# A gated linear recurrence and a two-layer MLP on one core: all steps issued in another order

## The chip, the core and the metric

The kernel runs on one core of a Trainium2 chip. The metric is the device time of one execution in microseconds; a version's time is the median of its executions. The core has five instruction queues that matter here: PE (TensorE, matrix products), DVE (VectorE) and ACT (ScalarE) for elementwise work, POOL (GpSimd) for small elementwise work, and SP (SyncE), which in this kernel issues every DMA transfer. Each queue runs its instructions in the order in which they were written; between queues, semaphores hold an instruction back until its inputs are there and its buffer is free.

## The reference

```python
# q, k, v, a_re, a_im: (4, 8, 768, 48), that is batch, heads, tokens, width
mag = np.sqrt(a_re * a_re + a_im * a_im)
scale = np.minimum(mag, 0.999) / (mag + 1e-06)
a_re_n, a_im_n = (a_re * scale, a_im * scale)
for t in range(S):
    new_re = ar * S_re - ai * S_im          # ar, ai: row t of a_re_n, a_im_n
    new_im = ar * S_im + ai * S_re
    S_re, S_im = (new_re + kv, new_im)      # kv: outer product of k[t] and v[t]
    y[:, :, t] = np.einsum('bhd,bhde->bhe', q[:, :, t], S_re)
# y reshaped to x: (3072 tokens, 384)
h = x @ w_in                                # w_in: (384, 2048)
g = np.maximum(h, 0.0) + alpha * np.minimum(h, 0.0)
out = g @ w_out                             # w_out: (2048, 384)
```

A recurrence with a complex gate per token and channel gives y; an MLP with a leaky rectifier is applied to every token of y.

## The kernel before, in words

**Units and stages.** The tokens are cut into 24 chunks of 128 (4 batches of 6), called units. The kernel is a set of Python generators, each a chain of steps, and each step writes one or a few instructions into one engine's queue:

- nine generators `gates` (letters A to I in the order; three for batch 0, two for each later batch). A gate generator loads the complex gates of one to three chunks (L248), computes decays and phases on ACT, DVE and POOL (L251 to L425: running products in L336 and L338, the decay tree in L316) and writes them to DRAM: the decays to `decs` (L321), the phases to `phs` (L417, L427).
- `loads` (J): for each unit the queries and keys KQ (L575, L577; three buffers), the phases PP (L586; one buffer) and the decays T (L593; two buffers).
- `half_rows` (K), which rearranges the values in DRAM into `vsc` (L556), and `loads_v` (L): the values V and VL of each unit (L602 to L628).
- `pieces` (M), `weights("in")` (N) and `weights("out")` (O): the MLP's weights are loaded as raw words (L487) and converted on ACT and DVE (L503 to L515).
- 24 generators `unit` (P to Z, then a to m). DVE turns KQ by the phases (L648). Then come six levels: PE makes the products `ps_lv` (L662) of queries with a copy W of the keys (L719 on ACT), DVE multiplies KQ by the decays T (L701), and the products are masked into A (L683 on ACT, L686 on DVE). Then KQ is transposed (L736), kv products are made (L747), y is summed from the levels (L759, L768) and from the state St (L777, L780 on DVE; L793 on PE), copied out (L807) and written to DRAM (`ysc`, L812). The first unit of a batch (P, V, b, h) loads its first state (L706) and scales it (L709).
- `loads_x` (n): reads y back as xT for a group of one or two units (L825; 14 groups). `all_mlp` (o): for each group and each of 16 feature blocks the product h (L841, three matmuls), the rectifier (L848 on ACT, L850 on DVE), and the output product (L860), two output rows of chunks; the result goes through L870 and out by L873.

A level of a unit needs DVE, PE and ACT one after another; the MLP of a group needs PE most. MLP steps of earlier groups are put between the levels of later units.

**What sets the order.** The string `ORDER` (L30 to L74) has one letter for each step, 4316 in all. `Plan.run` takes the letters from left to right and advances the generator of that letter by one step. So ORDER alone sets the order of every queue: a letter writes its instructions behind all that stand before it on the same engine. The calls `DVE(...)`, `ACT(...)`, `PE(...)`, `DMA(...)` in the yields (for instance `k_ = yield DVE(H * D, ek)` in L779, a step's size and what it waits for) were read by the planner that made the string; in the kernel they all go to a function that returns None. Semaphores are placed by the framework from the tiles that are read and written, whatever the order. The DMA issues of all generators stand in SP's one queue; the listing of the built program shows that an issue also waits for the transfer eight issues earlier, since eight semaphores are used in turn.

Of the kernel before, what the change touches and what calls it, by code (L numbers as in the profile page):

```python
# [27 lines left out]


ORDER = (  # L30
    "AAAAAAAAAAAAAAAAAAAABBJBAAMMMMKMAAAAAAANNBAAAAAAAAAAAAAAABNBMAAAJAAAAAAAAAAJJBANALBABAABANBBBOBABBAB"
    "AABAAAAKAOBNABKKMBBOBBOKBBBLLLAOABBLLLLLLABMLLBABANAAAAABOABABNAAABAKBAABNNOBBBNBBBONOMLBBBBOBOBBBBB"
    "BBNBBBBNNBOBBNBBNOOOBBBBOBCBJJPCBBBBBBOBMCCCOPBJBJCBMJNBPMBNNPPBBBJPKKKKKKKKBBBCBBCBOCKCBCBCCCCPCPCK"
    "BPCPPOPJJJLJCCPNJJPNPCDDCCCCPPCPOCONCQPCOPCQPPPQPPPQPCPPQCQOCJPJPPJPPMJJNPNNNCQCQQCCOOPPPPPCPOCPCNCP"
    "PPCPNCOPCPPCJMQQLPCCQQCDCOJPCCNNMLDCONCCCCCNCCNJKMCMnKKRCCCKORNCNCJCRLJJDCCCRCCCCQCOOOCCRRCCQCOCOOMO"
    "COOCRRooooNCNKKoCooNooOKCOCLKKMKoKKDCoooCCCCooQQQQKCooRQQCCQQNQQooQDooDDLLCNoooCDQQCQoQoooooRoooQDDQ"
    "DDRLLLLLLLLDDDoDoRQRDDDCQDQDQQQRDQRJQQQEEooooRDRoooRQNEJJJoQQNQQJJQDDLDDDDSDRDROoEoooooooESSRDSDooRo"
    "NoDERRoNRoDoSDREEooooSDLLLooEDooooRRoSLLLRDDDDRooORRDDSDDEQLLLLLLLRSRDRRNRRRRDSRDDDDODDooooDDDDEoNES"
    "oJooooOSSNJJEoJRJRRRSSTLLLLLLLLooSSoooOoJRRKDDJRoELSTnOTTToSKKoDDDoooooTLoSDDDDDDDDDoSSSSoRLToEooKoT"
    "oSoooooSSoSooooooooTETDEooSLoSSLLoETDDDEDDDooooooDSoooSSSSSSTSoSJTSoDEJJEJJEKJDoooLJLDoDLLEDEEoLoSSE"  # L40
    "SSSSSTSoooJoUoTEEEEooDDooToDooooEooooooooTnLDDooooDooooooooDEUTooooooJJLDDJooooDoooEoooooooooUTooToo"
    "oLLLLLooTDTETLooooooUTEooUoTTEoDUoooTEoEUTLooTKooEUEToJToToooUETTTTTTTETEEEETJEEEFJFETUoLoUUooooooUV"
    "TLUoFoToooTTLLUUooLoToUooVFVoUoUUUUoUUoooooFoJJUUVLLTULLLLLLoooVEEEUFUVooUUUEEEooTooEEEEEEEEEEEUUVUU"
    "UJUVUVEEFooVEooooJJJJJWVooEEEEEJUoUUUVooWUVJVoUVWKWJUoUVoEVEVWoVEEJoEEEoJWWWoJJJoVVVoWVooooVWEWVVnoL"
    "LLLLoVXLLLLooooLLLEEFLVFELEEEEFoEoVooooooVVoEoWEoVoooVoooVVVVVVVVWVEVLWWWooooooJoFFWVFWWEWXFooVVWWEV"
    "WooVLLJLJVooooooooooLLLLLVFWEWWFWWFoooooooWooooVWWoooWLLLLLWWWWWoFXXFXXWEWWoFoWFXXJFJJJJLYXFoooooooo"
    "XFXXoFFFFKJJWGoWWWXooooFooooYYWYXGWWWFoXFooYXFXoooooFoYXXXYFooYFFGFoooooooooXXooYXXooXYGooFXooFXFFXo"
    "oooXXGooXXFFFoFFLnooGoGJYoGLLLLLLLLLLLLXXXXXFFFXXFFFFXFFXJYJJJJZoGoooKooYoGooJoooooooooGGoYXZYYGYFFF"
    "FFFFFFGGJZFoZoFoooZoooGGooooXYYYYXXYZZZooYYLFLLLLLLooLLLFFoLoLLZooooXXYKKFFFFYYFFZYoooooGYYoFooFFFYF"
    "LoFGYGGGFooKoJJJKKFGGGGoYYYYYYYYYJXZooooKZoJJaKKKooLFFFooZZZLoJoZLLLooFGJLLLLXLLoLoKGFFFFoFFoooooooG"  # L50
    "GGYFYZaZaaZZooZZooooGaZZFLLFJFoooooooYYYYYYooaaFoaooooaoooJooJooZaZZZaooooZoooFZnZGGaooaoGooGGooZZZZ"
    "ZZZZaZZZGJJJHaaGJbbHooooooooooooooobGaGoZGZZaaaaaJLJJabGGHZoGZZZJJbooooooGGGooGooooaLooJboaabbHHboLL"
    "ooooaboaHbLaooaooooooHooLLLoLLooLaaLLoooGGooGGbaaGGaaGGaaooGoaJGoGGGGGGGGGGGHabbcLLHaHbGcbHHHHJJJboo"
    "ooooooooJJboooobLLGGocoobobJoooobcGGGcbbbboooHoHGbccbcKJJLLLLGoooooaocLdHaLooaobaGGbcLbLKLooGGLabbba"
    "ooooooobbGbbcHbGbbboocncoooHbGGGGGGGooocHHbodoooJJoLLoHLLoLLGGGLLLGLLHoooooLLoHooHoHoooooccKdooooooH"
    "HHHHGoooooHHooodoGLHcdoocccccobbbbbbHbdJdooGooooHoodHcHdoooooooocccddocoHHHodHHJcJJJoooJcoooccocIooo"
    "odHccccccoHccdIcoodeoHJoHoodooHHHHdodHddddHccccHJeLcLJcoooLJLLLeooooooooddooccLeLJoHHooHeHHHHHHHHedd"
    "dLIeoLooodooHHddooooLLdoLLoJJdeHHHdddddIIdddonoILJodoeoooooeLooILLfoooHHHHHHoeeooJooJIooKKoooooeHHfd"
    "dfIfodLeoeLKeKfoKKoeoodoLddIdLJJffLLLLLLeeofoeeIoofeooeooooIeooIofHHIJHHIdoIIeeooJoooHHHooeKHHoIIeoe"
    "ooeeeofHHoooeHHHHeeeeeIHLILLoooeIoeJeJJffooooooooooooKeoffgJffooooooIIoooooooooLLHHooIHHIIIfeeeeegoo"  # L60
    "ofoooeegooooooooLfffffooooooofgfggJooofLfJooLfooLLfLKHgLofLLgoofogJoffffffffIgffnooogogooJJJhIIIIooL"
    "oooIIhogoohJoooohIgLfJffLLgooooofffoIggoooooooooohLhLLLIgghgIggJLgLLgJooIooooggohgoIoIghofoooooohhgI"
    "IogoIIhgooohooooooLIIILIggggggggIJJhJooJhhgLLLhhiohoooooooIIoooohhhhhooooohohJooJgIIIIIIhhLLLIIIILhI"
    "IiooLooggooggihhhIoiooogoooooohIIIILIgJLLLLLoohoooooioIIooIIIIoIoohhohhhhhhihJoJnJiiiJJJJooooooooohI"
    "IIIIIIiooIjooIIoIIioiooIoooIIIooooojijiiooooooooLoojiooooIoojhLiILLiLLIoLoooiiiiJoLLooLooohLhooooIho"
    "ihhihjjooiooooiioiijjoooiiojiLLLioiiiioooJJJjjiiiioooLoooJjjioojjojJokooooooooojjikiiijjjJJkLoooijoo"
    "oookokkjjLkoooLookojkojkoojiijjnooookojoooooooookjLLLoLooLLLLLLjjjjjJJJkJJjJLoooooLLLLLoojjjoooooooo"
    "ooooolJJLoooollLjjjkjjojkkloooooooooooooooljjLkkkkklkLkllkJooooooooooolllkLklkJJLJLoooooolLkooookook"
    "kkooooooookkkkkkkkkJJoomooooooookkmkkkloollooooooJJokmooookknloooooooooommlmLoollmlLlloooooooloLoooo"
    "ooooooomoLllmmLLLooooooooolooooooooooollloooolloooomLoLoLLLLLllllllmlmmmoomoooooooooooooollmooooolll"  # L70
    "lllmomlmmmmmLooooooooLLoLLLoooLLLooLooooooooooooooooooooooooooooooooolnooooooomooooooooooooooooomooo"
    "ooooooooooooomoooomoomooooLooLLoomooooooooommooommmmmmmmmmmmmmmnoooooooooooooooooooooooooooooooooooo"
    "oooooooooooooooooooooooooooooooooooooooooooooooooooooooooooooooooooooooooooooooooooooooooooooooooooo"
    "oooooooooooooooo")  # L74

# [27 lines left out]
def kernel(  # L103
# [33 lines left out]
    B, HP, _, D, S = q.shape  # L137
    H = 2 * HP
# [60 lines left out]
    DVE = ACT = POOL = PE = DMA = step  # L199
# [443 lines left out]
    def unit(u):  # L643
# [59 lines left out]
        if c == 0:  # L703
            k_ = yield DMA(144, *[("state", u - 2)] * (u > 1), takes=(R["St"],))
# [3 lines left out]
            k_ = yield DVE(H * D, k_, ("start", 0))  # L708
            nc.vector.tensor_tensor(out=St, in0=St, in1=start[:, b].unsqueeze(2).to_broadcast([D2, H, D]), op=ALU.mult)  # L709
            state[b] = (St, k_)  # L710
        k_ = r
        for h in LEVELS:
# [12 lines left out]
            k_ = yield DVE(2 * H * HC, e, *[("decays", u)] * (h == 1))  # L725
# [23 lines left out]
        ek = e  # L749
# [23 lines left out]
        for s in range(1 if last else 2):  # L773
            before, known = states[s]
            k_ = yield DVE(H * D, known, takes=(R["St"],))
            St = work.tile([D2, H, D], F32, tag="St", name="St", bufs=3)
            nc.vector.tensor_tensor(out=St, in0=before, in1=T[:, :, TL - 4 + s:TL - 3 + s].to_broadcast([D2, H, D]),  # L777
                                    op=ALU.mult)
            k_ = yield DVE(H * D, ek)  # L779
            nc.vector.tensor_tensor(out=St, in0=St, in1=kv[s][0:D2], op=ALU.add)  # L780
            R["lv" if s else "misc"].put(k_)
            states.append((St, k_))
# [119 lines left out]
    with tc.manual_schedule():  # L902
        for i, g in enumerate(GATES):
            plan.add(gates(i, *g))
        plan.add(loads())
        plan.add(half_rows())
        plan.add(loads_v())
        plan.add(pieces())
        plan.add(weights("in"))
        plan.add(weights("out"))  # L910
        for u in range(NU):
            plan.add(unit(u))
        plan.add(loads_x())
        plan.add(all_mlp())
        plan.run(ORDER)
# [37 lines left out]
```

## Time and profile before

| | us |
|---|---|
| median of 3 executions | 864.73 |
| lowest and highest | 863.57, 866.52 |
| the profiled execution, its own time | 865.47 |
| its span, first to last instruction | 863.5 |
| busy: PE | 707.2 |
| busy: DVE | 649.0 |
| busy: ACT | 427.4 |
| busy: POOL | 172.2 |
| DMA: 129.20 MB on SP's queue, share of 16 engines | 65.1% |

The profile is of one execution. A busy time is the time in which at least one instruction of the engine was executing; the matmuls' ends are modelled, so a busy PE is not PE at its peak. The slices of the page cut the span in 40 equal parts of 21.6 us and give the busy share of each in tenths. A wait is named by the instruction that waited, the one that released it, the total in us, how many times, and the longest. Lines (L...) are those of the kernel file. A matmul of 32-bit floats shows as two records.

### The profile page before, as it was taken

The numbers are of one execution on the slowest core, as the hardware profiler recorded it, in microseconds if no ns is written. First come the engines' busy times: TensorE is split into PE (matmuls) and PEld (weight loads), VectorE is DVE, ScalarE is ACT, GpSimd is POOL, SyncE is SP. The second block draws the span as 40 slices with busy tenths as digits, with TensorE's granted clock in tenths as the row PEclk, the third lists the DMA queues.
The fourth block names the chain that finished last, engine by engine and source line by source line (L and its number), as shares of the span: only waits on it lengthen the run. The fifth ranks groups of instructions, "written<-read, shape, count | busy, mean of one in ns | idle before, by whom it ended". The sixth has DMA issues, their size and how long they took to land.

```text
span 863.5 us, 26876 instructions
## 1 busy us (share of the span) xinstructions
PE 707.2 (82%) x11488; PEld 528.3 (61%) x11488; DVE 649.0 (75%) x1012; ACT 427.4 (50%) x913; POOL 172.2 (20%) x277
## 2 busy tenths in 40 slices
PE   0001425777999899999899999998999999999998
PEld 0000424556776676776577777776777777777776
DVE  5989999897988989999679977977748655532212
ACT  7777585756455555743565355633333324223221
POOL 4000000066233300850345063110231000000000
PEclk9999957789999999999999999999999999999999
DMA  7699996875889587589865877667574674312010
GB/s 208 170 239 194 267 249 173 213 159 114 217 181 209 119 174 209 124 162 232 178 138 115 229 155 170 133 167 172 112 153 108 128 157 99 76 38 49 26 38 9
DMA packets 194559, 130.92 MB, mean 152 GB/s; under 512 B 74504, under 2 KB 186248, under 8 KB 194440
## 3 DMA queue, kind: packets, MB, share of 16 engines
q1 hardware_dynamic: 194440, 129.20, 65.1%
q8 instruction: 90, 1.47, 0.8%
q14 instruction: 29, 0.24, 0.1%
HBM read 100.82 MB, written 35.71 MB: 158 GB/s over the span
## 4 chain that ended last, share of the span: by engine, by line
PE 61%; DVE 16%; DMA 11%; issue 3%; SPq 3%; POOL 3%; ACT 2%; DVEq 0%; ACTq 0%; POOLq 0%
PE ps_h L841 24%; PE ps_o L860 24%; DMA T<-decs 5%; PE ps_lv L662 4%; DVE KQ L701 4%; PE ps_y L768 3%; PE ps_kv L747 2%; DMA phs<-gate 2%; PE ps_y L793 2%; DVE gate L336 2%; POOL gate L336 1%; PE ps_kt L736 1%; SPq L625 1%; DVE gate L422 1%; DVE gate L338 1%
## 5 line engine op out<-in xcount | busy, mean ns | idle before, releaser
L841 PE MATMUL ps_h<-xT,w_in_sb 128*128 128x256 f32 (+1 forms) x1344 | 308.7, 361 | 8.3 <-DVE g_sb L850 5.6
L860 PE MATMUL ps_o<-w_out_sb,g_sb 128*128 128x384 f32 x768 | 296.9, 501 | 13.4 <-DVE g_sb L850 6.6
L841 PEld LDWEIGHTS ps_h<-xT,w_in_sb 128*128 128x128 f32 x1344 | 235.0, 196 | 78.9 <-DVE g_sb L850 8.5
L701 DVE TENSOR_TENSOR KQ<-KQ,T 96x1024 f32<-96x1024 f32 x144 | 176.4, 1234 | 43.1 <-PE ps_lv L662 35.9
L848 ACT ACTIVATE g_sb<-ps_h 128x256 f32<-128x256 f32 (+1 forms) x224 | 79.0, 353 | 246.2 <-PE ps_h L841 245.4
L850 DVE SCALAR_TENSOR_TENSOR g_sb<-g_sb,al,ps_h 128x256 f32<-128x256 f32 (+1 forms) x224 | 97.3, 437 | 120.3 <-ACT g_sb L848 119.7
L860 PEld LDWEIGHTS ps_o<-w_out_sb,g_sb 128*128 128x128 f32 x768 | 138.1, 193 | 66.4 <-DVE g_sb L850 11.2
L662 PE MATMUL ps_lv<-KQ,W 96*32 96x32 f32 x3840 | 56.4, 205 | 50.4 <-ACT W L719 44.4
L719 ACT COPY W<-KQ 96x512 f32<-96x512 f32 x120 | 73.8, 623 | 43.1 <-DVE KQ L701 42.4
L662 PEld LDWEIGHTS ps_lv<-KQ,W 96*32 96x32 f32 x3840 | 44.6, 117 | 76.0 <-ACT W L719 52.5
L662 PE MATMUL ps_lv<-KQ 96*32 96x32 f32 x768 | 12.2, 208 | 71.2 <-DVE KQ L648 55.5
L648 DVE TENSOR_TENSOR KQ<-KQ,PP 96x2048 f32<-96x2048 f32 x24 | 56.3, 2344 | 12.8 <-DMA PP<-phs 12.7
L336 POOL TENSOR_TENSOR gate<-gate 128x72 f32<-128x72 f32 x42 | 29.6, 705 | 153.8 <-ACT gate L366 151.0
L662 PEld LDWEIGHTS ps_lv<-KQ 96*32 96x32 f32 x768 | 9.7, 120 | 75.0 <-DVE KQ L648 55.5
L683 ACT ACTIVATE A<-ps_lv,rows 128x64 f32<-128x64 f32 x144 | 40.3, 330 | 20.1 <-PE ps_lv L662 19.7
L336 DVE TENSOR_TENSOR gate<-gate 128x576 f32<-128x576 f32 (+5 forms) x84 | 47.4, 565 | 1.3
L768 PE MATMUL ps_y<-A,VL 64*48 64x64 f32 x2304 | 41.4, 224 | 5.2 <-DMA VL<-vsc 4.0
L422 DVE TENSOR_TENSOR gate<-gate 128x1152 f32<-128x1152 f32 (+2 forms) x36 | 43.3, 1216 | 0.8 <-POOL gate L407 0.7
L768 PEld LDWEIGHTS ps_y<-A,VL 64*48 64x48 f32 x2304 | 39.5, 125 | 5.7 <-DMA VL<-vsc 4.2
L807 ACT COPY yT<-ps_y 48x256 f32<-48x256 f32 x96 | 31.3, 365 | 20.4 <-PE ps_y L793 19.1
L686 DVE TENSOR_TENSOR A<-ps_lv,mask 128x256 f32<-128x256 f32 x96 | 39.5, 413 | 0.0
L780 DVE TENSOR_TENSOR St<-St,ps_kv 96x384 f32<-96x384 f32 x44 | 24.1, 548 | 15.3 <-PE ps_kv L747 12.4
(100 smaller groups left out, 766.6 us busy)
## 6 DMA issues: line engine op xcount, KB each, us to landing
T<-decs SPq DMA_DIRECT2D x48, 384.0 KB
PP<-phs SPq DMA_DIRECT2D x48, 193.5 KB
KQ<-in_q_dram SPq DMA_DIRECT2D x48, 192.0 KB
decs<-gate SPq DMA_DIRECT2D x7, 1152.0 KB
phs<-gate SPq DMA_DIRECT2D x14, 576.0 KB
KQ<-in_k_dram SPq DMA_DIRECT2D x40, 192.0 KB
vsc<-in_v_dram SPq DMA_DIRECT2D x48, 144.0 KB
VL<-vsc SPq DMA_DIRECT2D x24, 288.0 KB
```

Source lines behind the costliest of these rows:

```text
L336: on(4 * k).tensor_tensor(out=m, in0=w[:, 1::-1].unsqueeze(2).to_broadcast([P, 2, 2, k]), in1=pairs_of(u), op=ALU.mult)
L422: TT(out=m[:, a], in0=U5[:, 1 + a], in1=turned(off3, o)[:, a].unsqueeze(1).unsqueeze(3).to_broadcast([P, L // 2, nb, 2]), op=ALU.mult)
L648: nc.vector.tensor_tensor(out=KQ, in0=KQ, in1=bass.AP(tensor=PP.tensor, offset=PP.offset, ap=[PP.ap[0], (1, 2), (P + 1, H), (1, P)]), op=A ...
L662: nc.tensor.matmul(t[64 * i + j:64 * i + j + HC // 2, p], lhsT=weights(4 * i + p)[:, j:j + HC // 2], rhs=q_[:, m * g:m * (g + 1)], start=T ...
L683: nc.scalar.activation(a[:, :, cols], t[:, :, at:at + name], AF.Copy, scale=s)
L701: nc.vector.tensor_tensor(out=x, in0=x, in1=m, op=ALU.mult)
L719: nc.scalar.copy(W.rearrange("p n t -> p (n t)").rearrange("p (m h) -> p m h", h=h), halves(KQ[:, 1].rearrange("p n t -> p (n t)"), h)[:, ...
L768: nc.tensor.matmul(o, lhsT=Vp[h][64 * i:64 * i + 64, s, e_ * D:(e_ + 1) * D], rhs=a, start=False, stop=False)
L841: nc.tensor.matmul(p, lhsT=w_in_sb[:, f // 2, kk, f % 2 * P:(f % 2 + 1) * P], rhs=x_of[m][:, kk], start=(kk == 0), stop=(kk == NK - 1))
L848: nc.scalar.activation(gt, p, AF.Relu, scale=-1.0)
L850: nc.vector.scalar_tensor_tensor(out=gt, in0=gt, scalar=al_1[:, f:f + 1], in1=p, op0=ALU.mult, op1=ALU.add)
L860: nc.tensor.matmul(sums[0], lhsT=gt[:, c * P:(c + 1) * P], rhs=w_out_sb[:, f], start=(f == 0), stop=(f == NF - 1))
```

## The change

The string ORDER is replaced; the step counts of every letter are the same. The planner that made the new string took transfers as coming late by a random time, and bandwidths by packet size, among its durations. The only other edit adds an argument in L779, in a call that the kernel ignores.

```diff
 ORDER = (
-    "AAAAAAAAAAAAAAAAAAAABBJBAAMMMMKMAAAAAAANNBAAAAAAAAAAAAAAABNBMAAAJAAAAAAAAAAJJBANALBABAABANBBBOBABBAB"
-    "AABAAAAKAOBNABKKMBBOBBOKBBBLLLAOABBLLLLLLABMLLBABANAAAAABOABABNAAABAKBAABNNOBBBNBBBONOMLBBBBOBOBBBBB"
...
+    "AAAAAAAAAAAMMMMAABBAMMNAAAAAAAAAAAAAANBNNJJAJJBLAAAAAAALAALLLLLABAALLLAOAABAMAAAAAAAAAAAAAABBAANAAAA"
+    "BAABAAAAABBAOBBBABBAABABAOOBAAALBBBBAMBAABABAAABAOAAKBBBBBBBBKKKOOOOBKBBBKBOBBBBBONKJBJBBBBBBBBNNNKN"
...
@@ -776,7 +776,7 @@
-            k_ = yield DVE(H * D, ek)
+            k_ = yield DVE(H * D, ek, k_)
```

On SP the first rows become: the gates of A, the first tokens and alpha (L464, L467), the first raw weights, the gates of B, two more raw weights, KQ of P; the first `vsc` copies (L556), which stood among these, come after A's phases. P's T loads (L593) stand behind both gate loads of C in either order; before, a raw weight load and P's St lay between these and T, now P's St and two VL pieces come ahead of the gate loads, and T directly follows them. Q's PP and T are issued earlier with respect to Q's first step. On DVE, A's gate ends with less other work ahead (B's steps and the first weight conversions come later), and the conversions of the output weights are spread out further. From there on all queues differ nearly everywhere.

## The prediction

> **What bounds the kernel now.** First the page's busy times and slices, for the stages:
>
> ```profile
> PE 707.2 (82%) x11488; PEld 528.3 (61%) x11488; DVE 649.0 (75%) x1012; ACT 427.4 (50%) x913; POOL 172.2 (20%) x277
> ...
> PE   0001425777999899999899999998999999999998
> ...
> DVE  5989999897988989999679977977748655532212
> ...
> PEclk9999957789999999999999999999999999999999
> ```
>
> No engine is busy all the time, but one of two always is: DVE for the first 18 slices (to about 390 us), PE from slice 11 on. So I asked for the busy time by stage:
>
> ```profile
> 0.00:216.00 216.00, 81.89 (x1866) 64.35 (x1866) 192.69 (x377) 148.80 (x244) 39.43 (x76) 0.87 0.82 199
> 216.00:397.00 181.00, 170.05 (x2971) 126.22 (x2970) 165.50 (x219) 97.66 (x222) 59.79 (x85) 1.00 0.78 176
> 397.00:604.00 207.00, 199.37 (x3264) 147.51 (x3263) 168.03 (x228) 101.47 (x226) 57.37 (x81) 0.98 0.74 167
> 604.00:863.50 259.50, 255.88 (x3397) 190.21 (x3395) 122.81 (x192) 79.50 (x222) 15.60 (x35) 1.00 0.38 83
> ```
>
> The columns after the stretch and its length are PE, PE loads, DVE, ACT, POOL, granted clock, DMA share, GB/s. PE lacks 134 us of the first stage, then only 11.0, 7.6 and 3.6. DVE lacks 23.3 and 15.5 in the first two. So no order can take away much more than the 22 us of PE after 216 us, unless it shortens the first stage, and there DVE has little left.
>
> Next, what ended DVE's idle time before 397 us:
>
> ```profile
> DVE KQ L701 <- PE ps_lv L662: 7.2, 9, 1.5
> DVE KQ L648 <- DMA PP<-phs: 6.7, 4, 2.2
> DVE g_sb L850 <- ACT g_sb L848: 6.1, 5, 3.2
> DVE gate L257 <- ACT gate L255: 5.5, 1, 5.5
> DVE KQ L701 <- DMA T<-decs: 2.6, 2, 1.8
> ...
> DVE KQ L701 <- DMA VL<-in_v_dram: 1.4, 1, 1.4
> ```
>
> Late transfers cost DVE 6.7 + 2.6 + 1.4 = 10.7 us there (20.0 us over the whole span: PP 12.7, T 3.5, St 2.4, VL 1.4). After it, the chain of work that ended last shows one such place; PE's gap ends at 424.56:
>
> ```profile
> 400.36 6.99 DMA phs<-gate
> ...
> 408.82 9.06 DMA St<-in_v_dram
> ...
> 417.97 0.55 DVE St L709
> ...
> 424.56 1.83 PE ps_h L841 x4
> ```
>
> **The Trainium skill.** "Perfetto Trace Analysis", section Optimization Strategy, says that kernels can have several regimes with different most-contended engines and that interleaving them may help: the slices agree, and this order already interleaves them. "DMA: Bandwidth & Descriptors", section Latency and other measured facts, gives the HBM access as 0.2 us on average and 2 us at high load; the trace agrees that a transfer's time varies, since T of one size took 5.4 to 13.0 us on the chain. The same page, Issuing engines are not separate DMA queues, says that all transfers share 16 engines: so a large load ahead of a small one matters (DMA share 0.64 to 1.06 in the first slices). "TensorE: Matmul & The Clock Gate", section What's actually happening, says that idle windows of some 3.4 us halve the clock; the trace has PE gaps of 9.4 and 4.4 us before 121 us, and the clock at 0.58 to 0.92 from 108 to 216 us.
>
> **The change, part by part.** It adds and removes no instruction: every generator's steps are the same in number, only their interleaving differs; the added argument in L779 goes to a function that ignores it, so it costs nothing. I therefore worked with places: I walked each engine's old and new order and added up the trace's own duration of every instruction ahead. On DVE all 1012 add up to 704 us. Durations overlap (35.8 us up to 397 us) about as much as DVE idles (38.8), so the place is nearly the time: Z's last decay product has 395.6 us ahead and started at 398.3, U's L648 215.3 and started at 216.2. For PE I took the usual distance from one start to the next by kind (431 ns for L841 with 256 columns, 221 with 128, 645 for L860, and so on): 625.9 us in both orders. From 440.6 to 840.4 us the trace went forward 399.8 us while these sums went forward 369.1; less a stall of 4.9 us that is 1.07, which I apply.
>
> (1) *The two engines against each other.* For each DVE instruction that a matmul waits for: DVE work up to its end, plus 1.07 times the PE work from that matmul on. Before, the largest sum is 845.5 (396.8 + 448.6, Z's last L701); after, 844.2 (331.4 + 512.8, X's fourth L701). The new order gives -1.3 us. It comes down to the same peak though A's gate ends 5.3 us earlier in the DVE order (29.3 against 34.6) and T's rotation stands 8.7 us later (199.7 against 191.0).
>
> (2) *Room ahead of the transfers.* For each unit's loads I took the DVE work (past 398 us PE's) between the place of the last DMA issue and its first reader. Of 138 such groups, 43 have under 2 us before, 25 after; the median goes from 4.8 to 7.8 us. Applied to waits that the trace shows:
> - PP of Q, S, Y: room 8.1 to 16.6, 1.0 to 7.7, 0 to 13.6; waits 1.17 + 2.20 + 2.08. T of S: 6.1 to 15.3; 0.79. Together 6.2 us, all where DVE sets the pace, so it counts fully. W's PP (1.29) keeps room 0; a's 1.40 and P's T (1.83) stay.
> - PP of b, 0 to 12.2: 2.3 us, part of the 3.85 us gap of PE before 424.6.
> - xT of the ninth token group, 0 to 6.9: PE idled 2.8 us of the slice from 582.9 to 604.5.
> Gain with (1): 1.3 + 6.2 + 2.3 + 2.8 = 12.6 us.
>
> (3) *Room lost.* P's T still stands behind both of C's gate loads (574.5 KB each), though no longer behind a raw weight of 768 KB, and its room goes from 3.7 to 0: up to 3.7 us more, at DVE's pace, with everything of P and Q behind it; at best nothing, since L648 and thus PP come earlier too. PP of X, d, e go to under 2 us. Before, 13 PP loads stood so and cost 12.7 us, 1.0 each: 3 us. j and l lose room too, but there DVE's sum is 35 us and more below the peak, so it hides there. b's St goes from 4.9 to 1.8 us, 3.1 us more, hidden behind the 3.5 us by which the sums of b (840.7) lie under the peak; without that cover it costs 3. Loss: 6.7 us.
>
> On SP every transfer also stands behind all earlier ones: xT of the first group now has 14.1 us after P's last matmul where it had 25.0 (taken: 19.8, while 12.0 was enough for the twelfth). Bounds: nothing, if the new queue lets it through in 12; 6 us if it takes 19.8 again. I take 0: PE's sum at that place (800 us) lies 44 below the peak; DVE would have to wait for Q's levels behind it.
>
> Sum: -12.6 + 6.7 = -5.9 us. On the profiled execution's 863.5 us of span that is 857.6, and its own time was 865.47, 2 us around the span; so 859.6 for such an execution. Against the median, 864.73 - 5.9 = 858.8.
>
> **Rivals.**
> - *DVE and PE interlock (slower).* In the new order the sum of (1) lies within 841.6 to 844.2 from DVE place 237 to 419; before, it rose from 833.1 at 240 to 845.5. So both engines lose all slack for 180 us, with 42 decay products (7 units x 6) that need a level product from a PE queue full of L841 and L860 ahead of it. Such a wait was 0.8 us (7.2 in 9). At 0.3 us more for each of the 42, 12.6 us: 864.7 - 5.9 + 12.6 = 871.4. It decides from 8.5 us (5.9 + 2.6), 0.2 each. For it: ps_lv is DVE's longest wait already. Against it: every PE place from 160 us of work on has the same DVE work ahead within 6 us.
> - *Hidden anyway (no change; also: the change does not do what it says).* The rooms are places, not times; SP may run ahead, as with V's St (room 0, no wait). Then only (1) is left, less P's T: -1.3 + 3.7, and part of (2): 864, in a range of 862.2 to 867.3.
> - *All late transfers vanish.* 20.0 us of DVE, but PE can win only what it idles: 1.3 + 11.0 (second stage) + 2.8 = 15: 849.6.
>
> **How the numbers follow.** A measurement tells about 0.3% (2.6 us) from no change. Forecast (851.5 to 862.1 us): 0.48. All vanish (under 851.5): 0.15. Hidden: 0.14. Interlock or another wait past 867.3: 0.23. Faster 0.63, same 0.14, slower 0.23. The range reaches 847 (17.7 us less, four fifths of what PE idles after 216 us) and 869 (more than half of the interlock's way): about 0.2 is left out. The forecast's own range is 851.5 to 862.1.
>
> **What would show it.** Right: PP waits of S, Y and b gone from DVE's waits; L648 of P near 47 us; X's fourth L701 near 330 us; PE's idle time after 216 us down from 22 to about 14; no PE gap near 424 or 585. Wrong: L701 waiting for ps_lv well over 7 us before 397 us, P's T over 6 us late, L648 of Z later than 350 us, or PE standing before the first L841 while Q's levels wait behind it.

## The result

| | before | changed |
|---|---|---|
| median, first comparison (20 executions each) | 863.58 | 862.12 |
| lowest and highest | 859.26, 866.85 | 856.77, 865.6 |
| the profiled execution, its own time | 865.47 | 863.12 |
| its span | 863.5 | 861.3 |

The ratio is 0.998 (95%: 0.996 to 0.9999), and the medians differ by 1.5 us; the forecast was 5.9 us less. Two later comparisons gave 0.9983 (0.9957 to 1.0009) and 0.9986 (0.9967 to 1.0005). So the change is worth 1.2 to 1.7 us by the ratios, less than the 0.3% that I took as what a measurement can tell, and two of the three intervals reach 1. A ratio here is worked out from the fast executions of both kernels and can differ by some tenths of a percent from the ratio of the medians beside it.

The page of the changed kernel, busy times and slices:

```profile
PE 706.0 (82%) x11488; PEld 528.0 (61%) x11488; DVE 651.1 (76%) x1012; ACT 428.8 (50%) x913; POOL 160.0 (19%) x277
...
PE   0000416758799899989999999999999999999998
...
DVE  5999999979978897979979888788668646334112
...
PEclk9999957889999999999999999999999999999999
```

From slice 19 on PE has a 9 in every slice but the last; before, slices 20 and 28 had an 8. In the first half it is no better than before. The busy time by stage says the same (columns as in the prediction: PE, PE loads, DVE, ACT, POOL, clock, DMA share, GB/s):

```profile
0.00:216.00 216.00, 79.49 (x1805) 62.01 (x1806) 197.61 (x383) 148.58 (x242) 43.37 (x80) 0.89 0.81 201
216.00:397.00 181.00, 168.26 (x3007) 124.96 (x3006) 155.20 (x202) 97.14 (x221) 45.27 (x78) 0.98 0.79 172
397.00:604.00 207.00, 204.99 (x3300) 152.03 (x3299) 175.34 (x238) 103.97 (x234) 52.00 (x84) 1.00 0.74 167
604.00:861.30 257.30, 253.31 (x3382) 188.98 (x3380) 122.92 (x192) 79.14 (x217) 19.35 (x35) 1.00 0.38 85
```

PE lacks 136.5, 12.7, 2.0 and 4.0 us; before, 134.1, 11.0, 7.6 and 3.6. PE's saving is in the third stage, and the first two have lost 4. What ended DVE's idle time before 397 us:

```profile
DVE KQ L701 <- PE ps_lv L662: 17.8, 13, 4.0
DVE g_sb L850 <- ACT g_sb L848: 8.7, 13, 1.7
...
DVE KQ L648 <- DMA vsc<-in_v_dram: 2.5, 1, 2.5
...
DVE KQ L701 <- DMA T<-decs: 0.7, 1, 0.7
```

Late transfers went from 10.7 to 3.2 us. (The 2.5 is X's L648 at 292.6 us. The view names a vsc copy, which L648 does not read; I take it for a wait for PP, issued at 286.4 us.) But the decay products waited 17.8 us for level products from PE, where they had waited 7.2, and L850 waited 8.7 for a rectifier on ACT, which itself follows PE, where it had waited 6.1. Up to 397 us DVE gained 7.5 us on transfers and lost 13.2 on these two.

The second trace of the changed kernel showed the same: 15.0 us for ps_lv, 1.9 for late PP and T, and a gap of 4.04 us near 190 us at the same instruction. A third had 20.4 us for ps_lv and no late PP or T.

### The profile page after: what moved, and what is told of

The parts are those of the page before. It is cut to its first block, busy times and chain, and to the rows that moved or that the text cites. A ratio compares the mean times of both kernels' runs of the same rounds, so it can differ in the third digit from the quotient of the medians.

```text
span 861.3 us, 26850 instructions
## 1 busy us (share of the span) xinstructions
PE 706.0 (82%) x11488; PEld 528.0 (61%) x11488; DVE 651.1 (76%) x1012; ACT 428.8 (50%) x913; POOL 160.0 (19%) x277
## 3 DMA queue, kind: packets, MB, share of 16 engines
HBM read 100.82 MB, written 35.71 MB: 159 GB/s over the span
## 4 chain that ended last, share of the span: by engine, by line
PE 68%; DVE 17%; DMA 4%; issue 3%; ACT 3%; SPq 2%; POOL 2%; DVEq 0%; ACTq 0%
PE ps_o L860 27%; PE ps_h L841 27%; PE ps_lv L662 5%; DVE KQ L701 3%; PE ps_y L768 3%; PE ps_y L793 2%; DVE gate L336 2%; PE ps_kv L747 2%; PE ps_kt L736 2%; DVE KQ L648 2%; DVE gate L338 1%; DMA VL<-vsc 1%; DVE gate L422 1%; POOL gate L336 1%; POOL gate L338 1%
## 5 line engine op out<-in xcount | busy, mean ns | idle before, releaser
L701 DVE TENSOR_TENSOR KQ<-KQ,T 96x1024 f32<-96x1024 f32 x144 | 176.5, 1234 | 46.5 <-PE ps_lv L662 43.9
L850 DVE SCALAR_TENSOR_TENSOR g_sb<-g_sb,al,ps_h 128x256 f32<-128x256 f32 (+1 forms) x224 | 97.3, 437 | 130.2 <-ACT g_sb L848 129.7
L848 ACT ACTIVATE g_sb<-ps_h 128x256 f32<-128x256 f32 (+1 forms) x224 | 78.7, 352 | 229.5 <-PE ps_h L841 228.3
L662 PE MATMUL ps_lv<-KQ,W 96*32 96x32 f32 x3840 | 55.9, 203 | 68.2 <-ACT W L719 64.0
L662 PEld LDWEIGHTS ps_lv<-KQ,W 96*32 96x32 f32 x3840 | 43.9, 115 | 92.6 <-ACT W L719 70.9
L719 ACT COPY W<-KQ 96x512 f32<-96x512 f32 x120 | 74.4, 624 | 47.0 <-DVE KQ L701 42.5
L648 DVE TENSOR_TENSOR KQ<-KQ,PP 96x2048 f32<-96x2048 f32 x24 | 54.8, 2283 | 5.5 <-DMA PP<-phs 3.1
L662 PE MATMUL ps_lv<-KQ 96*32 96x32 f32 x768 | 11.7, 204 | 53.4 <-DVE KQ L648 51.1
L336 POOL TENSOR_TENSOR gate<-gate 128x72 f32<-128x72 f32 x42 | 27.1, 645 | 151.0 <-ACT gate L366 122.3
L662 PEld LDWEIGHTS ps_lv<-KQ 96*32 96x32 f32 x768 | 9.2, 117 | 57.0 <-DVE KQ L648 50.3
L738 ACT COPY KT<-ps_kt 128x384 f32<-128x384 f32 x48 | 22.9, 478 | 28.5 <-PE ps_kt L736 28.2
```

Source lines behind the costliest of these rows:

```text
L336: on(4 * k).tensor_tensor(out=m, in0=w[:, 1::-1].unsqueeze(2).to_broadcast([P, 2, 2, k]), in1=pairs_of(u), op=ALU.mult)
L648: nc.vector.tensor_tensor(out=KQ, in0=KQ, in1=bass.AP(tensor=PP.tensor, offset=PP.offset, ap=[PP.ap[0], (1, 2), (P + 1, H), (1, P)]), op=A ...
L662: nc.tensor.matmul(t[64 * i + j:64 * i + j + HC // 2, p], lhsT=weights(4 * i + p)[:, j:j + HC // 2], rhs=q_[:, m * g:m * (g + 1)], start=T ...
L701: nc.vector.tensor_tensor(out=x, in0=x, in1=m, op=ALU.mult)
L719: nc.scalar.copy(W.rearrange("p n t -> p (n t)").rearrange("p (m h) -> p m h", h=h), halves(KQ[:, 1].rearrange("p n t -> p (n t)"), h)[:, ...
L848: nc.scalar.activation(gt, p, AF.Relu, scale=-1.0)
```

## Experiments

All kernels are compared with the kernel before on the same chip, and kernels of one set with each other. Where a kernel has six or eight lines more, its L707 and L709 are L701, its L856 is L850, its L668 is L662, and so on.

**More room in the old order.** Only the letters of `loads` and `loads_x` (J, n) moved up, by at most 30 places. Rooms by place (the DVE work between the last issue of a load and its first reader) under 2 us went from 43 to 15, the median from 4.8 to about 7.8 us, much as in the new order.

```diff
 ORDER = (   # step k of J (loads) and n (loads_x) up to 30 letters earlier
-    ... 22 to 30 steps of other generators, J0, J1, ...
+    ... J0, J1, ... 22 to 30 steps of other generators
```

(The three lines show the pattern; the string itself is longer.)

> The order before, with only the letters of the loads (J) and of xT (n) moved up, by at most 30 letters and never ahead of what they wait for; all steps of compute keep their order. Groups of loads with under 2 us of room: 43 before, 26 in the changed order, 15 here. Theory 1 (the changed order's early loads did save DVE time, and its order of compute steps gave it back, because PE falls behind between 216 and 258 us and DVE then waits for ps_lv): here only the first half happens, so DVE's waits for transfers up to 397 us fall from 10.7 to 4 us or less, its waits for ps_lv stay at 7 to 10 us, and the time falls by 4 to 8 us, ratio 0.991 to 0.995. Theory 2 (a late transfer is hidden anyway, because DVE would wait for PE next): the waits for transfers fall as much, those for ps_lv rise by about as much, to 13 us or more, and the ratio is 0.997 to 1.002.

Measured: 889.48 us, ratio 1.024 (1.0182 to 1.0298); the executions spread from 877.8 to 895.8. Both expectations missed, on the slow side. DVE's late PP before 397 us did fall, from 6.7 to 1.8. SP's and PE's waits in this kernel show the price:

```profile
SPq L593 <- DVE St L777: 55.6, 16, 6.9
...
SPq L575 <- PE ps_y L793: 32.9, 12, 5.2
...
PE ps_y L768 <- DMA VL<-vsc: 21.8, 8, 5.1
```

SP waited 23.4 us for T's buffer before, now 55.6; 13.9 for KQ's buffer, now 32.9. Behind these issues stand all others in SP's only queue: PE's wait for VL went from 4.0 to 21.8 us. So here room by place was not room in time: loads put ahead of the release of their buffers stopped SP, and the loads behind them came later.

**The halves of the two orders.** The first 2065 letters of the old order (in its trace to about 398 us) with the rest in the new one, and the first 2040 of the new (to about 399 us) with the rest in the old.

```diff
-ORDER = changed
+ORDER = before[:2065] + (what is left of the letters, in the changed order)
```

> The first 2065 letters of the order before (in its trace up to about 398 us), then what is left in the order of the changed kernel. Theory 1 (the changed order loses in its first half and wins in its second): first half as before, 398.0 us at 205 us of PE work, second half as changed, 861.3 - 405.4 = 455.9 us, together 853.9 us of span, 9.6 us less than before, ratio 0.989 (0.986 to 0.994). Theory 3 (the second half of the changed order only wins back what its own first half had put off, so the halves can't be parted): no better than the changed kernel, ratio 0.996 to 1.000.

> The counterpart: the first 2040 letters of the changed order (in its trace up to about 399 us), then what is left in the order before. Theory 1: 399.4 us at 200 us of PE work plus 863.5 - 392.7 = 470.8 us, together 870.2 us of span, ratio 1.008 (1.004 to 1.011). Theory 3: ratio 0.998 to 1.002.

Measured: 861.95 us, ratio 0.9983 (0.996 to 1.0006), and 866.4 us, 1.0016 (0.9991 to 1.004). Both lie in theory 3's ranges: the halves cannot simply be parted. The values become useful beside the same pair without loads, below.

**One stop on ScalarE.** DVE's longest wait for a level product in the changed kernel, 4.04 us from 187.5 us, is for one of S. Its copy W (L719 on ACT) stood behind a step of gate D (L364), which waited for POOL. The edit puts the copy ahead (S8 is the ninth step of unit S, and so on):

```diff
-  J34 n1 D60 o82 J35 D61 D62 D63 D64 D65 D66 S8 D67 K29
+  J34 n1 S8 D60 o82 J35 D61 D62 D63 D64 D65 D66 D67 K29
```

> The changed order with one letter moved: the step that copies S's keys for its level 4 (W, on ACT) is put ahead of the two steps of gate D (L364, L366, on ACT) that wait for POOL, which it stood behind. In the changed kernel's trace ACT stood there from 185.0 to 189.8 us, PE 4.9 us and DVE 4.0 us. Theory 1 (up to there DVE sets the pace and what it loses is passed on): the gap of 4.0 us at 187.5 goes, and the time falls by 2 to 4 us against the changed kernel, ratio to the kernel before 0.993 to 0.996. Theory 2 (another wait takes its place): the gap goes, the time stays within 1 us of the changed kernel's, ratio 0.997 to 0.999.

Measured: 860.09 us, ratio 0.9939 (0.9921 to 0.9957), in theory 1's range and 2.0 us under the changed kernel's first median. In the trace T's L648 starts at 195.4 instead of 198.2 us and the first reader of the last xT at 830.5 instead of 834.3. Since these two times are of different sets, I ran both again side by side:

> The changed kernel with S's copy of W ahead of gate D on ScalarE, again, beside the changed kernel on the same chip. Nothing is left out. Theory 1 (the stop at S's copy counts, about 2 us): 1.5 to 3 us under the changed kernel of this set, ratio to before 0.992 to 0.9965. Theory 2 (its gain was chance, as moving a level product ahead as well gave 0.9987): within 1 us of the changed kernel.

> The changed kernel a third time, unedited, for its time on the same chip and a third trace. Ratio 0.996 to 1.000; DVE's waits for ps_lv before 397 us 13 to 19 us; PE's waits for its own issue 8 to 12 us in all (11.0 and 8.1 in the two traces before; 18.8 in the kernel before).

Measured: 859.23 us, ratio 0.9965 (0.9945 to 0.9984), and 859.89 us, 0.9986 (0.9967 to 1.0005). The medians are only 0.7 us apart, which is theory 2; the ratios differ by 0.0021, 1.8 us, at the edge of theory 1. ps_lv waits before 397 us were 14.2 us against 20.4 (I had expected 13 to 19 for the latter), waits for the rectifier (L850 for L848) 11.5 against 8.0. So the stop is worth 0.7 to 2 us of its 4; in the one set that has both kernels the difference is within noise. This is the fastest kernel here that leaves nothing out: below the kernel before in both comparisons, below the changed one by less than its interval.

**The same kind of stop in the old order.** There ACT stands at the same steps of D from 191.6 to 197.1 us, and DVE has a gap of 3.25 us.

```diff
-  ... T4 o89 S18 K30 K31 o90 D62 D63 D64 o91 ... o95 T5 ...    (D60, D61 further ahead)
+  ... T4 o89 S18 K30 K31 o90 o91 ... o95 T5 D60 D61 D62 D63 D64 ...
```

> The kernel before with one edit: the five steps of gate D that stood on ScalarE at 191.6 us, waiting for GpSimd until 197.1, go behind the step of T whose copy (L719) and the L848 stood behind them. Nothing is left out. Theory 1 (a stall of DVE in the first 397 us counts in full, as one did in the new order): the DVE gap of 3.25 us at 196.2 goes, time ratio 0.9950 to 0.9975, and T's and U's later steps start 2 to 4 us earlier. Theory 2 (the two engines wait for each other again a little later, so that a stall taken away comes back): ratio 0.9985 to 1.0015, with DVE's waits for ps_lv before 397 us up by 2 to 3 us from 7.2.

Measured: 863.25 us, ratio 1.0007 (0.9984 to 1.003): theory 2. U's L648 started 2.7 us earlier (213.5 against 216.2), but W's L648 came at 270.7, against 270.1: the gain was given back within 55 us, and ps_lv's waits rose from 7.2 to 10.8 us.

**PP and T out of the way, in both orders.** This was the decisive set. Each kernel loads PP and T once, for the first unit, and uses them for all 24: it leaves out the rotations and decays of units 1 to 23, and 92 loads with their bytes.

```diff
-                if i == 0:
-                    L["PP"] = PP = work.tile([D2, H, P + 1], F32, tag="PP", name="PP", bufs=1)
-                nc.sync.dma_start(PP[rows], ...)
+                if u == 0:
+                    if i == 0:
+                        kept["PP"] = work.tile([D2, H, P + 1], F32, tag="PP", name="PP", bufs=1)
+                    PP = kept["PP"]
+                    nc.sync.dma_start(PP[rows], ...)
+            L["PP"] = kept["PP"]          # and T in the same way
```

> The kernel before with PP and T loaded once, for the first unit, and kept: 46 PP and 46 T loads are gone, and no unit after the first waits for a rotation or decay. Left out: the rotations and decays of units 1 to 23 (every unit takes the first one's). Gates and their writes stay. Theory 1 (late PP and T count in full, as the forecast summed them): before 397 us DVE loses 6.7 + 2.6 us to them, b's PP 2.3 more; the ratio is 0.986 to 0.991. Theory 2 (where a transfer comes in time, DVE waits for PE in its place): ratio 0.995 to 1.000, and DVE's waits for ps_lv before 397 us rise from 7.2 to 12 or more. Theory 3 (the single SP queue matters most: without 92 loads V, xT and the weights come sooner): ratio below 0.986, and PE's waits for VL and xT nearly gone.

> The same edit in the changed kernel: PP and T loaded once and kept. Left out: the rotations and decays of units 1 to 23. Theory 1: its late PP and T were only 2.5 + 0.7 us before 397 us, so it gains about 3 us: ratio to before 0.993 to 0.996, which leaves it 3 to 8 us behind the kernel before with the same edit. Theory 2: both gain 0 to 3 us and lie within 2.5 us of each other. Theory 3: both gain over 8 us.

> The changed kernel again, nothing edited, for its ratio on the same chip as the kernels with kept PP and T and for a second trace. Ratio 0.996 to 1.000. Waits that belong to the order come again: late PP, T and VL cost DVE under 5 us before 397 us (3.2 in the first trace), ps_lv 13 to 20 us (17.8), and the gap of DVE near 190 us, behind gate D's steps on ScalarE, is 3 to 5 us. If they were chance, ps_lv's waits would fall to under 10 or the gap near 190 be under 2.

| same set | with its loads | PP and T kept | the loads cost |
|---|---|---|---|
| order before | 863.83 | 841.75 | 22.1 |
| changed order | 860.82 | 852.09 | 8.7 |
| changed less before | -3.0 | +10.3 | -13.4 |

The ratios to before are 0.976 (0.973 to 0.9791), 0.9882 (0.9851 to 0.9913) and, for the changed kernel, 0.9983; by them the loads cost 20.7 and 8.7 us, and the three entries of the last row are -1.5, +10.5 and -12.0. No theory fits the first run (theory 1 said 0.986 to 0.991; theory 3 said below 0.986, but with PE's waits for VL and xT nearly gone, and they were 3.5 and 1.0 us), and the second gained more than theory 1 said. The finding: **the sign turns**. Without these loads the changed order is 10 us slower. The loads cost it 12 to 13 us less, and it pays 10 for that in the order of its other work.

Stages and DVE's waits before 397 us with PP and T kept, first of the order before:

```profile
0.00:216.00 216.00, 87.26 (x1916) 68.64 (x1916) 197.87 (x383) 151.01 (x253) 46.28 (x80) 0.89 0.68 176
216.00:397.00 181.00, 176.90 (x3227) 132.13 (x3228) 171.77 (x232) 98.22 (x221) 58.02 (x82) 1.00 0.59 150
```

```profile
DVE g_sb L856 <- ACT g_sb L854: 6.6, 7, 3.2
...
DVE KQ L707 <- PE ps_lv L668: 4.9, 8, 1.4
```

then of the changed order:

```profile
0.00:216.00 216.00, 80.62 (x1779) 62.95 (x1783) 196.29 (x381) 148.72 (x242) 42.77 (x80) 0.87 0.67 177
216.00:397.00 181.00, 176.03 (x3198) 132.38 (x3188) 163.79 (x215) 100.51 (x228) 46.46 (x82) 0.99 0.54 137
```

```profile
DVE KQ L707 <- PE ps_lv L668: 15.3, 13, 4.0
DVE g_sb L856 <- ACT g_sb L854: 7.1, 13, 1.7
```

ps_lv costs 15.3 us where the other order has 4.9, with no late load in sight: it belongs to the order. (Of the 15.3, 4.05 us is the stop at S's copy. Another 2.06 us is at R's product, at 150 us, in the middle of which PE stood 1.40 us for "issue", that is, for nothing that the profile shows.) Between these two traces PE's idle time differs by 6.7 us in all, 6.6 of it before 216 us.

A count of work makes the stages comparable. For each trace I added the usual distances of the prediction over the PE instructions started by 397 us, and DVE's durations likewise; what is left of PE's 625.9 us then takes the rest of the span:

| trace | PE work by 397 us | DVE work by 397 us | rest of PE's work | time for it | us per us |
|---|---|---|---|---|---|
| before | 204.7 | 394.3 | 421.2 | 466.5 | 1.108 |
| changed | 197.9 | 386.1 | 428.0 | 464.3 | 1.085 |
| before, kept | 215.5 | 406.9 | 410.4 | 443.5 | 1.081 |
| changed, kept | 205.6 | 395.5 | 420.3 | 452.4 | 1.076 |

At 397 us the changed kernel is *behind*, by 6.8 us of PE's work and 8.2 of DVE's; kept, by 9.9 and 11.4. It wins its time after that: at the rate before, its remaining 428.0 us would have taken 474.0, and they took 464.3. (The other two traces of the changed kernel have 201.5 and 200.9 us of PE work by 397, so they are behind by 3.2 and 3.8, and 1.085 and 1.084 after it.)

**Where in the order the 10 us lie.** The halves again, with PP and T kept.

```diff
-ORDER = changed                     # PP and T kept in all four
+ORDER = changed[:2040] + (the rest, in the order before)
+ORDER = before[:2065] + (the rest, in the changed order)
```

> PP and T kept as in the two kernels of the last set (left out: the rotations and decays of units 1 to 23), with the changed order for its first 2040 letters (about to 390 us) and the order before for the rest. Kept, the changed order ended 10.3 us behind the other. Theory 1 (the loss is in the first 390 us, where DVE waited 10.4 us longer for level products): 851 to 855 us, ratio to before 0.985 to 0.990, with DVE's waits for ps_lv before 397 us at 13 to 17 us. Theory 2 (it is in the rest of the order): 840 to 845 us, ratio 0.973 to 0.978. Theory 3 (the two halves can't be parted): 846 to 849 us.

> PP and T kept (left out: the rotations and decays of units 1 to 23), the order before for its first 2065 letters and the changed order for the rest. Theory 1: 839 to 844 us, ratio 0.972 to 0.977, ps_lv waits before 397 us at 4 to 7 us. Theory 2: 851 to 855 us. Theory 3: 846 to 849 us.

Measured: 856.18 us, ratio 0.9906 (0.9872 to 0.994), just above theory 1's interval, and 847.38 us, 0.9818 (0.9775 to 0.9861), in theory 3's. As ratios to before, first half in the rows:

| first half, rest: | before, before | before, changed | changed, before | changed, changed |
|---|---|---|---|---|
| with loads | 1 | 0.9983 | 1.0016 | 0.998 |
| PP and T kept | 0.976 | 0.9818 | 0.9906 | 0.9882 |

Averaged over the other half, the changed first half costs 9.1 us when loads are out of the way (0.0064 and 0.0146) and 0.6 with them (-0.0003 and 0.0016); the changed rest costs 1.5 us kept and saves 2.3 with loads. So the loss of the kept pair lies in the first 398 us. With loads the two effects, 0.6 and 2.3 us, are about the size of one ratio's interval (0.0024, some 2 us, each way): that the net gain lies after 398 us rests on the count of work above, and the halves agree with it without showing it. The halves do not add up: in the kept pair the two mixed orders are together 7.1 us slower than the two whole ones, some 3.5 us for each seam if both seams cost the same.

**Late data, or bytes?** PP and T kept, but their loads still issued: into DRAM, where nobody reads them; and then with 2 of their 48 rows.

```diff
-                    L["PP"] = PP = work.tile([D2, H, P + 1], F32, tag="PP", name="PP", bufs=1)
+                    PP = dram.tile([D2, H, P + 1], F32, tag="PPd", name="PPd") if u else kept["PP"]
                 nc.sync.dma_start(PP[rows], ...)      # and T in the same way
```

```diff
-                nc.sync.dma_start(PP[rows], phs[...][:, ...])
+                few = slice(0, 2 if u else D)
+                nc.sync.dma_start(PP[rows][few], phs[...][few, ...])
```

> The kernel before with PP and T kept from the first unit (left out: the rotations and decays of units 1 to 23), but the loads of units 1 to 23 still issued at their places, with the same bytes, into DRAM, where no instruction reads them. The traffic stays; the wait of L648 and L701 for the data and the wait of these loads for a free buffer go. Theory 1 (what cost the kernel before 22 us was that PP and T came late): 841 to 847 us, ratio 0.973 to 0.981. Theory 2 (it was the load on the 16 transfer engines, which made the other loads late): 854 to 864 us, ratio 0.989 to 1.000, with PE's waits for VL and xT over 6 us.

> The same edit in the changed kernel: PP and T kept (left out: the rotations and decays of units 1 to 23), their loads issued at their places into DRAM and unread. Theory 1: as with the loads gone, 851 to 855 us, ratio 0.985 to 0.990, so that the order before, with late PP and T taken out of both, stays 8 us or more ahead. Theory 2: 857 to 864 us, and the two orders lie within 4 us of each other.

> As the kernel before with its PP and T loads unread (left out: the rotations and decays of units 1 to 23), but each of those loads now takes 2 of its 48 rows. The 184 issues stay at their places in SP's queue; nearly all of their bytes go. Theory 1 (from 350 us on the bytes of these loads held back xT and other loads): 840 to 846 us, ratio 0.972 to 0.979, as with the loads gone. Theory 2 (it is their place in the one queue, with the wait of each issue for the one eight before it): 856 to 868 us, ratio 0.990 to 1.004.

Measured: 868.26 us, ratio 1.0057 (1.0031 to 1.0083); 870.13 us, 1.0066 (1.0038 to 1.0094); 843.35 us, 0.9772 (0.9741 to 0.9802). The last is theory 1 of its run: the issues in SP's queue (92, not the 184 that I had counted) cost 1 us by the ratios, within noise; in these kernels the bytes cost the rest. With unread loads both kernels came out above every theory's interval; the whole gain was gone. But not everywhere: up to 340 us the unread run went with the kept one (U's L648 at 210.9 against 211.1, Z's at 342.6 against 339.5; with read loads 216.2 and 349.7), so there 7 of the 10 us were waits for the data or for a free buffer in SBUF, which the unread loads do not have. Then it fell back. Two short stretches of the order before with unread loads:

```profile
402.00:408.00 6.00, 3.24 (x7) 2.50 (x8) 2.88 (x2) 0.28 (x1) 0.00 (x0) 0.52 1.04 150
408.00:414.00 6.00, 6.00 (x95) 4.10 (x94) 2.14 (x5) 2.51 (x9) 0.00 (x0) 0.91 0.99 294
```

The transfer engines are full (share 1.04), PE stood 4.34 us for xT from 400.4 to 404.8, and its clock was 0.52 and then 0.91. The two orders, 10.3 us apart with the loads gone, are 1.9 us apart (0.0009 in ratio) with the loads there and nobody waiting for them. So in these kernels most of the turn of the sign comes with the bytes, and not with a wait for PP or T. In both kernels the unread loads are written to DRAM (62.91 MB written, 35.71 with the loads read), so how the loss after 350 us, and the turn of the sign with it, divides between bytes and late data in the real kernel stays open.

**The level products moved ahead.** The copy of S as above, R's level product ahead of Q's kv products, and two of U and Z ahead of MLP products.

```diff
-  Q32 D20 D21 D22 Q33 ... Q41 o29 J27 R5        o209 ... o213 U17        o457 o458 o459 Z17
+  R5 Q32 D20 D21 D22 Q33 ... Q41 o29 J27        U17 o209 ... o213        Z17 o457 o458 o459
```

> The changed kernel with four steps moved ahead: S's copy of W ahead of gate D on ScalarE (as in the run that did this alone), R's level product ahead of Q's kv products on PE, and level products of U and Z ahead of a few MLP products. Nothing is left out. Theory 1 (waits for level products before 230 us count in full; later ones do not, since PE is then never idle): R's 2.06 and S's about 2 us, so 856.5 to 859.5 us where the changed kernel alone has 860.8 to 862.1; ratio to before 0.990 to 0.995. Theory 2 (each wait counts, the 1.4 us of U and Z too, and 2 us more): under 856.5. Theory 3 (only the copy counts): the ratio of the run with the copy alone, 0.9939, or above.

> The same four steps moved, with PP and T kept (left out: the rotations and decays of units 1 to 23). The changed order with PP and T kept took 852.1 us, 10.3 more than the order before. Theory 1: 847 to 849.5 us, ratio to before 0.979 to 0.984, with ps_lv waits of DVE before 397 us down from 15.3 to 10 to 12. Theory 2: 841 to 846 us. Theory 3 (waits for level products are not what sets the two orders apart): 851 to 853 us.

> S's copy of W ahead of gate D, with PP and T kept (left out: the rotations and decays of units 1 to 23). The changed order so was at 852.1 us. Theory 1: the stop counts here too, 849 to 851 us. Theory 2 (the two engines meet elsewhere, as when the level products were moved, which took 855.8): 852 us or more.

Measured: 863.81 us, ratio 0.9987 (0.996 to 1.0013); 855.77 us, 0.9905 (0.9878 to 0.9932); and with the copy alone 851.07 us, 0.9879 (0.9846 to 0.9912). The first is theory 3's, the second is slower than all three expected, and the copy alone lies 0.07 us above theory 1's interval, 1.0 under the kernel without it (0.3 by the ratios, which is within noise). With more moves there was no gain. DVE's waits before 397 us in the kept kernel with four moves:

```profile
DVE g_sb L856 <- ACT g_sb L854: 17.7, 16, 4.0
DVE KQ L707 <- PE ps_lv L668: 9.4, 10, 1.7
```

ps_lv fell from 15.3 to 9.4, and the rectifier's wait rose from 7.1 to 17.7. In this trace PE stood still from 148.0 us:

```profile
151.91 1.44 PE L847 MATMUL ps_h<-xT,w_in_sb 128*128 128x128 f32 x5 [3.94 <-issue]
```

In the kernel without moves R's product took 2.1 us there (150.1 to 152.2) instead of 0.5, with 1.40 us of "issue" in it; whatever is first in PE's queue then is late, and DVE waits for that. The wait is not one of level products alone: it is DVE waiting for PE, and part of it took another name when the queue was changed. The 2.5 us more of "issue" in the kernel with four moves are a rival for most of the 3.7 us by which it is slower than the kept kernel without moves; no run parts the two.

## Why the prediction was wrong

*The step that failed is (1).* It said "so the place is nearly the time", and from that "the new order gives -1.3 us". The place was nearly the time because DVE's overlaps (35.8 us) and idle time (38.8) cancelled, but 10.7 us of that idle time were the late transfers which step (2) then took away. With PP and T kept, Z's last decay product in the order before ended at 387.1 us, not at its place of 396.8. X's fourth in the changed order ended at 330.9, near its place of 331.4, since there DVE idles for PE instead. With these times the sums of the two peaks are 387.1 + 448.6 = 835.7 and 330.9 + 512.8 = 843.7. The new order costs 8.0 us, not -1.3; the kept traces are 8.9 us apart in span, the medians 10.3. So the late transfers were counted once in (1), as a later place of the old peak, and again in (2); and DVE's waits for PE in the new order, 15.3 us for ps_lv against 4.9 with PP and T kept, were a rival in the prediction and nothing in its sum.

*Steps (2) and (3), together -4.6 us, had the right sign and were too small: -13.4 by the medians, -12.0 by the ratios.* The two errors have opposite signs, some 10 us one way and some 8 the other; that their sum came within 5 us of the measured time is luck.
- Before 397 us the named waits went as said: PP of Q, S, Y and T of S are gone, 10.7 became 3.2. "All where DVE sets the pace, so it counts fully" was wrong. DVE is no further at 397 us than before, but 8.2 us behind: in place of the transfers it waited for PE.
- After it the sum had 2.3 (b) and 2.8 (ninth group) against 3.0 lost, 2.1 in all. At the two places PE's stalls are gone, and the rate of the rest shows 9.7 us (474.0 less 464.3). But the 2.8 us of the ninth group were misread. In the kernel before PE waited there 2.33 us on "issue" (the longest of the first line below) and 0.48 us for xT (the longer of the second):

```profile
PE ps_o L860 <- issue: 3.0, 3, 2.3
...
PE ps_h L841 <- DMA xT<-ysc: 0.7, 2, 0.5
```

  One term I had left out is the clock. The kernel before, from 420 us and from 582 us:

```profile
420.00:426.00 6.00, 2.15 (x7) 1.07 (x5) 4.87 (x8) 3.45 (x8) 1.28 (x5) 0.90 0.71 130
426.00:432.00 6.00, 6.00 (x84) 4.47 (x84) 4.60 (x6) 4.26 (x9) 5.45 (x8) 0.81 0.51 107
582.00:588.00 6.00, 3.93 (x110) 2.89 (x98) 4.34 (x6) 0.38 (x1) 0.00 (x0) 1.00 1.13 297
588.00:594.00 6.00, 5.25 (x14) 3.68 (x15) 4.49 (x7) 1.38 (x3) 0.00 (x0) 0.72 0.42 99
```

  and the changed kernel at the same times:

```profile
420.00:426.00 6.00, 6.00 (x90) 4.33 (x85) 5.81 (x8) 5.97 (x13) 2.81 (x3) 1.00 0.88 185
588.00:594.00 6.00, 6.00 (x101) 4.45 (x97) 5.90 (x11) 2.50 (x6) 0.00 (x0) 1.00 0.33 62
```

  Around these stalls PE's clock fell to 0.81 and 0.72 in the kernel before, and it stayed at 1.00 in the changed one, which has none there. If PE's work goes with the clock, that is 1.1 and 1.7 us of 6 more, an estimate from these four lines.
- P's T, 3.7 us lost: not so. P's L648 started at 48.0 us (said: 47), all waits for T before 397 us are 0.7 us. PP of X, d and e were to cost 3.0; X's cost 2.5 and e's 1.3, d's nothing.
- xT of the first group, taken as 0 between 0 and 6: PE waited 1.8 us for it at 117 us, where DVE sets the pace.

*Rivals.* The interlock happened where it was put: 10.6 us more of ps_lv before 397 us, over its point of 8.5. It did not make the kernel slower because the loads' term, 12 to 13 us, was nearly three times the 4.6 that it was set against. "Hidden anyway" had the time nearly right (864, 862.2 to 867.3) and the reason wrong: two terms of 10 and 12 to 13 us cancel. The late transfers did not all vanish.

*What was to show it.* Right: the PP waits of S, Y and b gone, P's L648, no PE gap near 424 or 585; X's fourth L701 started at 333.4 us (said: near 330). Wrong: PE's idle time after 216 us is 18.7 us, not about 14; and two of the named signs against it are there, ps_lv at 17.8 us and Z's L648 at 353.1.

## What to carry to other kernels

A place calibrated on a trace holds that trace's waits. Take the waits out before adding up an order's own work, or a gain is counted twice. To part an order from its transfers, run both orders with the suspected loads made once and kept: four kernels gave both terms, where all waits of the two profiles had given neither. Such a kernel takes away the bytes along with the waits, so a second one is needed to tell these apart. And when two engines are both near their bound, moving the instruction that is waited for may only rename the wait: four moves took 5.9 us off one and put 10.6 on another.

## What the runs showed of the hardware

**PE's waits for nothing that the profile shows.** The profile calls them "issue". The kernel before, page and PE's waits:

```profile
q8 instruction: 90, 1.47, 0.8%
```

```profile
PE ps_lv L662 <- issue: 12.1, 6, 3.7
...
PE ps_o L860 <- issue: 3.0, 3, 2.3
PE ps_h L841 <- issue: 2.0, 1, 2.0
...
PE ps_y L793 <- issue: 1.7, 1, 1.7
```

That is 18.8 us; in the changed kernel 11.0, 8.1 and 11.9 in three traces; with PP and T kept 4.6 and 4.2. Queue 8 brings 90 packets of 16 KB, one every 8 us while PE works. From the packet records of six traces, 19 of the 26 such waits over 0.9 us ended 1.1 to 1.9 us after one of these packets had landed; about 10% of all moments lie so. The Trainium skill, "Runtime: NRT & Kernel Launch", section Instruction fetch mechanics, says that instructions come in blocks of 16 KiB over a queue of the engine's own and that the cost is mostly hidden. The trace of the kernel before agrees as to the number, 11 waits beside 90 packets, but the 11 took 18.8 us. They may be blocks that came late while PP and T filled the transfer engines, and then a part of what the bytes cost. The link is a coincidence in time, not an experiment.

**POOL's small products took three times as long while DVE worked.** The chain of the changed kernel around the stop at S's copy:

```profile
176.97 1.79 POOL gate L336
...
180.24 3.38 POOL gate L336
...
185.02 0.52 POOL gate L336
...
187.67 0.33 POOL gate L336
...
188.40 0.33 POOL gate L336
```

One instruction on 128x72 took 0.33 us once DVE stood idle, from 187.5 us, and 0.5 to 3.4 before. Over the whole trace, the 12 of this form with DVE idle took 0.31 to 0.32 us, and the 18 with DVE busy for at least 95% of their time took 0.93 on average. The Trainium skill, "SBUF — State Buffer", section SBUF: two separate sides, says that VectorE and GpSimd share a pair of ports under an exclusive lock; the trace is in line with that, and no run here tests it. So the chain through POOL, which DVE waited for here, ran fast only once DVE had stopped.
